# Squared-relu attention and an ELU feed-forward on one core: the lo*lo product of the scores is left out, and its neighbour runs as 64-row matmuls

## The chip, the cores and the metric

The kernel runs on one core of a Trainium2 chip. The metric is the device time of one execution in microseconds (us), lower is better. TensorE (PE) does the matrix products; each matmul instruction first loads its stationary operand, the weights (PEld). ScalarE (ACT) and VectorE (DVE) do the elementwise work, and SyncE's queue (SP) issues the DMA transfers. PSUM is the memory that TensorE writes: eight banks, each of 512 float32 values in each of 128 partitions.

## The reference

Four batches of 3008 tokens go through attention without softmax, and the 12032 tokens then through a feed-forward part with 2048 hidden units.

```python
scores = (1 / S) * z @ z.T            # z: 4 x 3008 x 64
attn = np.maximum(scores, 0.0) ** 2
x = u * (attn @ v)                    # u, v: 4 x 3008 x 256
h = x @ w_in                          # 256 x 2048, float64 weights
g = np.where(h > 0, h, np.exp(np.minimum(h, 0)) - 1)
out = g @ w_out                       # 2048 x 256
```

## The kernel before

Each float32 operand of a product is split into two float32r halves of 12 significant bits, hi + lo. A product of two operands is then hi\*hi + hi\*lo + lo\*hi, three matmuls that accumulate in PSUM.

The queries of a batch are cut into six blocks (four of 502, two of 500), 24 blocks in all; the keys into 12 pairs of 128-key chunks per block. A step is one pair of one block: 288 steps in attention. In a step, `a_front` makes the scores of the pair in one score tile `f` (two banks, one for each chunk), `a_mid` makes relu and square on ScalarE and splits the result into `hi` and `lo` on VectorE, and two steps later `a_back` multiplies them with the values `v` into an accumulator `acc` (two banks, d = 0 and 1), twelve matmuls. After a block's last pair (p = 11) VectorE multiplies the accumulator with `u`, and the result `x` goes to DRAM.

Scores have only 64 rows (z has 64 features), so hi and lo of a key chunk lie one under the other in `l`: rows 0 to 63 hold hi, rows 64 to 127 hold lo. The queries are held twice: `hh` has hi in both halves of the rows, `ll` has lo in both. One matmul of `l` with `hh` gives hi\*hi + lo\*hi, one with `ll` gives hi\*lo + lo\*lo.

The feed-forward part has 24 blocks of 8 steps: `m_front` (12 matmuls into a tile `h` of the same kind as `f`), `m_mid1` to `m_mid4` on ScalarE and VectorE, and three steps later `m_back` (12 matmuls into an accumulator `yacc`, copied out by ScalarE at the block's end).

The order of work is written out by hand: a loop over slots t issues, for each t, `a_front(t)`, `a_mid(t)`, background jobs of that slot, then `a_back(t - 2)`. Every engine's queue has its work in that order. The background jobs are the loads and splits of the next operands: `v_split` and `l_hi`, `l_lo` (in 12 slots around each batch's start), `r_split` (hh and ll of the next block), `w_split` (the weights' hi and lo, one VectorE operation per slot over 128 slots).

In PSUM, `f` and `acc` have two buffers each of two banks, which are all eight.

Of the kernel before, what the change touches and what calls it, by code (L numbers as in the profile page):

```python
# [7 lines left out]
F32 = mybir.dt.float32  # L8
# [2 lines left out]
AF = mybir.ActivationFunctionType  # L11
ALU = mybir.AluOpType

# Every float32 operand of a matrix product is split exactly into two float32r
# halves of 12 significant bits (hi + lo); a product is then hi*hi + hi*lo + lo*hi
# in three single-pass float32r matmuls that accumulate in float32.
BLOCKS = (502, 502, 502, 502, 500, 500)


# [1 line left out]
def relu2_attention_elu_mlp(  # L21
# [9 lines left out]
    nc = tc.nc  # L31
    B, D, S = uT.shape
    K = zz.shape[1] // 2
    DFF = w_in.shape[1]
    P = 128
    KD = D // P
    KF = DFF // P
# [9 lines left out]
    MS = KF // 2  # L47
# [7 lines left out]
    z1 = ctx.enter_context(tc.tile_pool(name="z1", bufs=1))  # L55
    p2 = ctx.enter_context(tc.tile_pool(name="p2", bufs=2))
    p3 = ctx.enter_context(tc.tile_pool(name="p3", bufs=3))
    ps = ctx.enter_context(tc.tile_pool(name="ps", bufs=2, space=bass.MemoryType.PSUM))
    dr = ctx.enter_context(tc.tile_pool(name="dr", bufs=1, space=bass.MemoryType.DRAM))

    wi_hi = res.tile([P, KD, DFF], F32R, name="wi_hi")
# [7 lines left out]
    def sub(lo, src, hi):  # L69
        nc.vector.tensor_tensor(out=lo, in0=src, in1=hi.bitcast(F32), op=ALU.subtract)  # L70

    def copy(out, in_):
        nc.scalar.activation(out=out, in_=in_, func=AF.Copy)  # L73
# [2 lines left out]
        copy(hi, src)  # L76
        sub(lo, src, hi)

# [1 line left out]
    v_raw, v_t = {}, {}  # L80

    def v_load(b, p):
# [13 lines left out]
        split(o[:, 0], o[:, 1], t)  # L96
        v_t[b, p] = o

# [1 line left out]
    l_raw, l_t = {}, {}  # L100

    def l_load(b, g, c0=0, c1=GW):
# [11 lines left out]
        copy(l_t[b, g][:, c0:c1], l_raw[b, g][:, c0:c1])  # L114

    def l_lo(b, g, c0=0, c1=GW):
        o = l_t[b, g][K:, c0:c1]
        sub(o, l_raw[b, g][K:, c0:c1], o)

# [1 line left out]
    r_raw, r_t = {}, {}  # L121

    def r_load(k):
# [18 lines left out]
        nc.sync.dma_start(out=t[:, :, :n], in_=uT[b, :, i0:i0 + n].rearrange("(c p) n -> p c n", p=P))  # L142
        u_t[k] = t

    # ---- float64 weights: hi = the sign, the exponent and 11 bits of the fraction,
    # lo = the next 24 bits of it, rounded to 12. The exponent is rebased by dropping
    # three of its bits, which a magnitude in float32's range determines; smaller
    # magnitudes become zero. ----
    UNIT = 512
    WARM = 7  # L150
    w_raw = {}
# [44 lines left out]
        yield  # L196
        stt(out=lo, in0=r, scalar=2.0 ** -35, in1=h.bitcast(F32), op0=ALU.mult, op1=ALU.mult)

# [1 line left out]
    def products(late):  # L200
        if late:
            return [(c, d, q) for c in range(2) for q in (0, 2, 1) for d in range(KD)]
        return [(c, d, q) for c in range(2) for d in range(KD) for q in range(3)]

# [1 line left out]
    x_d = {}  # L206
    f_t, e_t, acc_t = {}, {}, {}

    def a_front(s):
        k, p = divmod(s, NP)  # L210
        n, b = cols(k)[1:]
        t = ps.tile([P, 2, 512], F32, tag="f", name="f")
        hh, ll = r_t[k]
        for c in range(2):
            o = (p % 4) * 2 * P + c * P
            w = l_t[b, p // 4][:, o:o + P]
            nc.tensor.matmul(t[:, c, :n], w, hh[:, :n], start=True, stop=False)  # L217
            nc.tensor.matmul(t[:, c, :n], w, ll[:, :n], start=False, stop=True)  # L218
        f_t[s] = t

    def a_mid(s):
        k, p = divmod(s, NP)
# [13 lines left out]
    def a_back(s):  # L236
        k, p = divmod(s, NP)
        n, b = cols(k)[1:]
        hi, lo = e_t.pop(s)
        vt = v_t[b, p]  # L240
        if p == 0:
            acc_t[k] = ps.tile([P, KD, 512], F32, tag="acc", name="acc")
        acc = acc_t[k]
        for c, d, q in products(s < 2):
            end = p == NP - 1 and c == 1
            if end and q == 1:
                continue
            w = vt[:, q // 2, c, d * P:(d + 1) * P]
            g = (lo if q == 1 else hi)[:, c, :n]
            nc.tensor.matmul(acc[:, d, :n], w, g, start=(p == 0 and c == 0 and q == 0), stop=(end and q == 2))  # L250
        if p == NP - 1:
            u = u_t.pop(k)
            nc.vector.tensor_tensor(out=u[:, :, :n], in0=acc_t.pop(k)[:, :, :n], in1=u[:, :, :n], op=ALU.mult)
            x_d[k] = dr.tile([P, KD, n], F32, name=f"x{k}")
            nc.sync.dma_start(out=x_d[k], in_=u[:, :, :n])

# [1 line left out]
    xr_t, x_t, g_t, y_t = {}, {}, {}, {}  # L258

    def x_load(k):  # L260
# [13 lines left out]
    def m_front(s):  # L274
        k, m = divmod(s, MS)
        n = cols(k)[1]
        hi, lo = x_t[k]
        t = ps.tile([P, 2, 512], F32, tag="f", name="h")
        for c in range(2):
            f0 = (2 * m + c) * P  # L280
            for j in range(KD):
                wh, wl = wi_hi[:, j, f0:f0 + P], wi_lo[:, j, f0:f0 + P]
                o = t[:, c, :n]
                nc.tensor.matmul(o, wh, hi[:, j, :n], start=(j == 0), stop=False)  # L284
                nc.tensor.matmul(o, wh, lo[:, j, :n], start=False, stop=False)  # L285
                nc.tensor.matmul(o, wl, hi[:, j, :n], start=False, stop=(j == KD - 1))  # L286
        f_t[s] = t
# [10 lines left out]
        nc.scalar.activation(out=h[:, c0:c1, :n], in_=f[:, c0:c1, :n], func=AF.Copy)  # L298
        nc.vector.tensor_scalar(out=m[:, c0:c1, :n], in0=h[:, c0:c1, :n], scalar1=0.0, scalar2=None, op0=ALU.min)  # L299

    # exp(m) - 1 = (exp(m) + 1) * tanh(m / 2), which keeps its digits near zero
    def m_mid2(s, c0=0, c1=2):
        n = cols(s // MS)[1]
        _, m, t = g_t[s]
# [26 lines left out]
    def m_back(s):  # L331
        k, m = divmod(s, MS)
        i0, n, b = cols(k)
        hi, lo = e_t.pop(s)
        if m == 0:
            acc_t[k] = ps.tile([P, KD, 512], F32, tag="acc", name="yacc")
        acc = acc_t[k]
        late = s >= MSTEP - 2
        for c, d, q in products(late):
            f = 2 * m + c  # L340
            w = (wo_lo if q == 2 else wo_hi)[:, f, d * P:(d + 1) * P]
            g = (lo if q == 1 else hi)[:, c, :n]
            nc.tensor.matmul(  # L343
                acc[:, d, :n], w, g, start=(f == 0 and q == 0), stop=(f == KF - 1 and q == (1 if late else 2))
            )
        if m == MS - 1:
            del acc_t[k]
            y = vp.tile([P, KD, NB], F32, tag="v", name="y")
            t0 = b * S + i0
            if s < MSTEP - 1:  # L350
                copy(y[:, :, :n], acc[:, :, :n])
                nc.sync.dma_start(
                    out=outT[:, t0:t0 + n].rearrange("(c p) n -> p c n", p=P), in_=y[:, :, :n]
                )
            else:
                copy(y[:, 0, :n], acc[:, 0, :n])
                nc.vector.tensor_copy(out=y[:, 1, :n], in_=acc[:, 1, :n])
                nc.sync.dma_start(out=outT[:P, t0:t0 + n], in_=y[:, 0, :n])
                nc.scalar.dma_start(out=outT[P:, t0:t0 + n], in_=y[:, 1, :n])

# [1 line left out]
    jobs = {}  # L362

    def at(slot, fn, *a):
# [41 lines left out]
    with tc.manual_schedule():  # L406
        l_load(0, 0, 0, 2 * P)
        r_load(0)
        l_load(0, 0, 2 * P, GW)
        warm = p3.tile([P, 512], F32R, tag="hi", name="warm")  # L410
        nc.vector.memset(warm.bitcast(F32), 0.0)
        copy(p3.tile([P, 1], F32R, tag="lo", name="cwarm"), warm[:, :1].bitcast(F32))
        f = ps.tile([P, 2, 512], F32, tag="f", name="fwarm")
        for i in range(WARM):
            nc.tensor.matmul(f[:, i % 2], warm[:, :P], warm, start=True, stop=True)
        l_hi(0, 0, 0, 2 * P)
        l_lo(0, 0, 0, 2 * P)
        r_split(0)
        l_hi(0, 0, 2 * P, GW)
        l_lo(0, 0, 2 * P, GW)  # L420
        for t in range(-9, 0):
            background(t)
        for t in range(NSTEP + MSTEP + 3):
            s = t - NSTEP
            if s < 0:
                a_front(t)
                a_mid(t)
            elif s < MSTEP:
                m_front(s)
                m_mid1(s)  # L430
            if 2 <= s < MSTEP:
                m_mid4(s - 2)
            if 0 <= s < MSTEP:
                m_mid2(s)
            if 1 <= s < MSTEP - 1:
                m_mid3(s - 1)
            if s == MSTEP - 1:
                halves = (0, 1), (1, 2)
                for fn, k in (m_mid3, s - 1), (m_mid4, s - 1), (m_mid3, s), (m_mid4, s):
                    for c0, c1 in halves:  # L440
                        fn(k, c0, c1)
            background(t)
            if t >= 2 and s < 2:
                a_back(t - 2)
            if s >= 3:
                m_back(s - 3)
        assert not jobs, sorted(jobs)
# [32 lines left out]
```

## Time and profile before

| | us |
|---|---|
| three runs, median (lowest to highest) | 2108.54 (2108.49 to 2109.82) |
| the profiled execution's span, first to last instruction | 2107.8 |
| PE busy / PEld busy | 2097.8 / 1729.8 |
| DVE busy / ACT busy | 1533.2 / 1437.1 |
| granted TensorE clock, mean | 0.999 |

The span is that of the one execution that was profiled; it has no device time of its own beside it, and the median of the runs lies 0.7 us above the span. Busy time of PE counts each matmul to its modelled end, and these overlap, so the pace of the matmuls is read from their starts.

### The profile page before, as it was taken

What the parts mean: (1) busy time and instruction counts of PE and PEld (TensorE: products, weight loads), DVE (VectorE), ACT (ScalarE), POOL (GpSimd) and SP (SyncE); (2) the same over time, 40 slices, a digit from 0 to 9 for tenths busy, and PEclk for the clock granted to TensorE, in tenths of its full rate; (3) what the DMA queues carried; (4) which work ended last, traced back from release to release, by engine and by line L of the source; (5) the groups of instructions that cost most, each with busy time, mean ns of one, the idle gap of its engine ahead of it and who ended that gap; (6) DMA issues with size and microseconds to landing.
All of it is one profiled execution on the core that took longest, in us unless ns stands there. A gap on an engine that the chain in (4) does not pass through costs nothing.

```text
span 2107.8 us, 22966 instructions
## 1 busy us (share of the span) xinstructions
PE 2097.8 (100%) x9175; PEld 1729.8 (82%) x9175; DVE 1533.2 (73%) x1648; ACT 1437.1 (68%) x1481; POOL 0.2 (0%) x4
## 2 busy tenths in 40 slices
PE   9999999999999999999999999999999999999998
PEld 7888888888888888888888888888888888888887
DVE  6767777677765576555587877777777877778777
ACT  7555665556655576555577777777777777777776
POOL 0000000000000000000000000000000000000000
PEclk9999999999999999999999999999999999999999
DMA  4121321113110031000101000000000000010000
GB/s 129 41 63 45 95 65 62 45 43 102 58 49 25 25 103 55 31 25 25 40 22 38 20 20 20 28 32 20 20 20 32 28 20 20 20 37 23 20 10 20
DMA packets 44555, 84.18 MB, mean 40 GB/s; under 512 B 3872, under 2 KB 35744, under 8 KB 44448
## 3 DMA queue, kind: packets, MB, share of 16 engines
q1 hardware_dynamic: 44304, 82.46, 12.1%
q8 instruction: 71, 1.16, 0.2%
q14 instruction: 36, 0.29, 0.0%
q10 hardware_dynamic: 144, 0.26, 0.0%
HBM read 58.06 MB, written 24.64 MB: 39 GB/s over the span
## 4 chain that ended last, share of the span: by engine, by line
PE 98%; DVE 0%; ACT 0%; DMA 0%; issue 0%; SPq 0%; DVEq 0%; ACTq 0%
PE acc L250 37%; PE yacc L343 25%; PE h L286 8%; PE h L284 8%; PE h L285 8%; PE f L218 6%; PE f L217 6%; DMA lraw<-in_zz 0%; ACT ghi L326 0%; DVE glo L327 0%; DVE hc L314 0%; ACT hc L298 0%; ACT l L73 0%; DVE t L311 0%; ACT r L229 0%
## 5 line engine op out<-in xcount | busy, mean ns | idle before, releaser
L250 PE MATMUL acc<-hi,v 128*128 128x502 f32 (+1 forms) x2304 | 752.2, 391 | 1.8 <-DVE v L70 1.1
L228 ACT ACTIVATE r<-f 128x1004 f32<-128x1004 f32 (+1 forms) x288 | 290.6, 1009 | 382.2 <-PE f L218 381.5
L250 PEld LDWEIGHTS acc<-hi,v 128*128 128x128 f32 x2304 | 434.3, 189 | 94.0 <-DVE v L70 1.5
L230 DVE CAST hi<-r 128x1004 fp32r<-128x1004 f32 (+1 forms) x288 | 196.5, 682 | 329.6 <-ACT r L229 329.1
L250 PE MATMUL acc<-lo,v 128*128 128x502 f32 (+1 forms) x1104 | 429.6, 390 | 0.1
L298 ACT ACTIVATE hc<-h 128x1004 f32<-128x1004 f32 (+1 forms) x192 | 193.8, 1009 | 249.1 <-PE h L286 249.0
L70 DVE TENSOR_TENSOR lo<-r,hi 128x1004 fp32r<-128x1004 f32 (+1 forms) x288 | 346.6, 1204 | 10.1
L229 ACT ACTIVATE r<-r 128x1004 f32<-128x1004 f32 (+1 forms) x288 | 300.3, 1043 | 9.1
L343 PE MATMUL yacc<-ghi,wo_hi 128*128 128x502 f32 (+1 forms) x768 | 299.9, 391 | 0.8 <-ACT ghi L326 0.8
L343 PE MATMUL yacc<-ghi,wo_lo 128*128 128x502 f32 (+1 forms) x768 | 300.1, 392 | 0.0
L343 PE MATMUL yacc<-glo,wo_hi 128*128 128x502 f32 (+1 forms) x768 | 298.8, 390 | 0.6 <-DVE glo L327 0.6
L284 PE MATMUL h<-xhi,wi_hi 128*128 128x502 f32 (+1 forms) x768 | 299.2, 390 | 0.0
L285 PE MATMUL h<-xlo,wi_hi 128*128 128x502 f32 (+1 forms) x768 | 298.8, 389 | 0.0
L286 PE MATMUL h<-xhi,wi_lo 128*128 128x502 f32 (+1 forms) x768 | 298.7, 389 | 0.0
L327 DVE TENSOR_TENSOR glo<-hc,ghi 128x1004 fp32r<-128x1004 f32 (+2 forms) x194 | 231.4, 1193 | 46.7 <-ACT ghi L326 46.5
L299 DVE TENSOR_SCALAR m<-hc 128x1004 f32<-128x1004 f32 (+1 forms) x192 | 130.9, 682 | 169.5 <-ACT hc L298 169.5
L250 PEld LDWEIGHTS acc<-lo,v 128*128 128x128 f32 x1104 | 208.6, 189 | 44.7 <-DVE lo L70 0.5
L314 DVE SCALAR_TENSOR_TENSOR hc<-hc,t 128x1004 f32<-128x1004 f32 (+2 forms) x194 | 231.3, 1192 | 6.6
L311 DVE SCALAR_TENSOR_TENSOR t<-m,t 128x1004 f32<-128x1004 f32 (+2 forms) x194 | 229.9, 1185 | 0.0
L217 PE MATMUL f<-hh,l 128*128 128x502 f32 (+1 forms) x576 | 224.8, 390 | 1.0 <-DVE l L70 0.8
L218 PE MATMUL f<-ll,l 128*128 128x502 f32 (+1 forms) x576 | 224.9, 390 | 0.0
L306 ACT ACTIVATE m<-m 128x1004 f32<-128x1004 f32 (+1 forms) x192 | 200.6, 1045 | 6.1
(42 smaller groups left out, 1800.0 us busy)
## 6 DMA issues: line engine op xcount, KB each, us to landing
vraw<-in_v SPq DMA_DIRECT2D x44, 256.0 KB, 2.7
u<-in_uT SPq DMA_DIRECT2D x16, 502.0 KB, 4.7
x<-u SPq DMA_DIRECT2D x16, 502.0 KB, 3.5
xr<-x SPq DMA_DIRECT2D x16, 502.0 KB, 4.2
outT<-y SPq DMA_DIRECT2D x16, 502.0 KB, 3.5
wraw<-in_w_in SPq DMA_DIRECT2D x8, 512.0 KB, 4.3
wraw<-in_w_out SPq DMA_DIRECT2D x8, 512.0 KB, 3.4
rraw<-in_zz SPq DMA_DIRECT2D x16, 251.0 KB, 4.7
```

What stands on the lines that cost most here:

```text
L70: nc.vector.tensor_tensor(out=lo, in0=src, in1=hi.bitcast(F32), op=ALU.subtract)
L217: nc.tensor.matmul(t[:, c, :n], w, hh[:, :n], start=True, stop=False)
L218: nc.tensor.matmul(t[:, c, :n], w, ll[:, :n], start=False, stop=True)
L228: nc.scalar.activation(out=r[:, :, :n], in_=f[:, :, :n], func=AF.Relu, scale=1.0 / S)
L229: nc.scalar.activation(out=r[:, :, :n], in_=r[:, :, :n], func=AF.Square)
L250: nc.tensor.matmul(acc[:, d, :n], w, g, start=(p == 0 and c == 0 and q == 0), stop=(end and q == 2))
L284: nc.tensor.matmul(o, wh, hi[:, j, :n], start=(j == 0), stop=False)
L285: nc.tensor.matmul(o, wh, lo[:, j, :n], start=False, stop=False)
L286: nc.tensor.matmul(o, wl, hi[:, j, :n], start=False, stop=(j == KD - 1))
L314: nc.vector.scalar_tensor_tensor(out=h[:, c0:c1, :n], in0=h[:, c0:c1, :n], scalar=0.0, in1=t[:, c0:c1, :n], op0=ALU.max, op1=ALU.add)
L327: nc.vector.tensor_tensor(out=lo[:, c0:c1, :n], in0=g[:, c0:c1, :n], in1=hi[:, c0:c1, :n].bitcast(F32), op=ALU.subtract)
L343: nc.tensor.matmul(acc[:, d, :n], w, g, start=(f == 0 and q == 0), stop=(f == KF - 1 and q == (1 if late else 2)))
```

## The change

The lo\*lo part of the scores is left out. In `l` the odd chunks have their halves exchanged: lo in rows 0 to 63, hi in rows 64 to 127. The matmul with `hh` uses all 128 rows as before. The one with `ll` uses the 64 rows that hold hi: the upper half of the rows for an even chunk, the lower for an odd one, as two matmuls of 64 rows that stand next to each other and write different banks. The score matmuls of two pairs are issued together in every second slot, four with `hh`, then four with `ll`. Score tiles get three buffers (six banks). The accumulator is now one, as two tiles of one bank, `acc0` and `acc1`, for d = 0 and 1; in a block's first and last pair the products are ordered by d first. The multiplication with u and the copy of y are made for each d apart. Comments were removed.

```diff
-    ps = ctx.enter_context(tc.tile_pool(name="ps", bufs=2, space=bass.MemoryType.PSUM))
+    pf = ctx.enter_context(tc.tile_pool(name="pf", bufs=3, space=bass.MemoryType.PSUM))
+    pa = ctx.enter_context(tc.tile_pool(name="pa", bufs=1, space=bass.MemoryType.PSUM))
...
     def l_lo(b, g, c0=0, c1=GW):
-        o = l_t[b, g][K:, c0:c1]
-        sub(o, l_raw[b, g][K:, c0:c1], o)
+        for c in range(2):
+            rows = slice(K, P) if c == 0 else slice(0, K)
+            o = l_t[b, g][rows, c0:c1].rearrange("p (n two w) -> p n two w", two=2, w=P)[:, :, c]
+            x = l_raw[b, g][rows, c0:c1].rearrange("p (n two w) -> p n two w", two=2, w=P)[:, :, c]
+            sub(o, x, o)
...
-    def products(late):
+    def products(late, edge):
         if late:
             return [(c, d, q) for c in range(2) for q in (0, 2, 1) for d in range(KD)]
+        if edge:
+            return [(c, d, q) for d in range(KD) for c in range(2) for q in range(3)]
         return [(c, d, q) for c in range(2) for d in range(KD) for q in range(3)]
+    def acc_tiles(k):
+        acc_t[k] = [pa.tile([P, 512], F32, tag=f"acc{d}", name=f"acc{d}") for d in range(KD)]
...
     def a_front(s):
         k, p = divmod(s, NP)
         n, b = cols(k)[1:]
-        t = ps.tile([P, 2, 512], F32, tag="f", name="f")
         hh, ll = r_t[k]
-        for c in range(2):
-            o = (p % 4) * 2 * P + c * P
-            w = l_t[b, p // 4][:, o:o + P]
-            nc.tensor.matmul(t[:, c, :n], w, hh[:, :n], start=True, stop=False)
-            nc.tensor.matmul(t[:, c, :n], w, ll[:, :n], start=False, stop=True)
-        f_t[s] = t
+        work = []
+        for i in range(2):
+            f_t[s + i] = pf.tile([P, 2, 512], F32, tag="f", name="f")
+            for c in range(2):
+                o = ((p + i) % 4) * 2 * P + c * P
+                work.append((f_t[s + i][:, c, :n], l_t[b, (p + i) // 4][:, o:o + P], c))
+        for t, w, c in work:
+            nc.tensor.matmul(t, w, hh[:, :n], start=True, stop=False)
+        for t, w, c in work:
+            rows = slice(c * K, (c + 1) * K)
+            nc.tensor.matmul(t, w[rows], ll[rows, :n], start=False, stop=True)
...
         if p == NP - 1:
             u = u_t.pop(k)
-            nc.vector.tensor_tensor(out=u[:, :, :n], in0=acc_t.pop(k)[:, :, :n], in1=u[:, :, :n], op=ALU.mult)
+            del acc_t[k]
+            for d in range(KD):
+                nc.vector.tensor_tensor(out=u[:, d, :n], in0=acc[d][:, :n], in1=u[:, d, :n], op=ALU.mult)
...
-                copy(y[:, :, :n], acc[:, :, :n])
+                for d in range(KD):
+                    copy(y[:, d, :n], acc[d][:, :n])
...
             if s < 0:
-                a_front(t)
+                if t % 2 == 0:
+                    a_front(t)
                 a_mid(t)
```

On PE, two steps within the second block stood like this before (f, hh, ll, l: scores and their operands; hi, v: the products' operands; the number is the tile's):

```order
L250 MATMUL acc_179<-hi_357,v_363 128x502
L217 MATMUL f_438<-hh_107,l_238 128x502
L218 MATMUL f_438<-ll_108,l_238 128x502
L217 MATMUL f_438<-hh_107,l_238 128x502
L218 MATMUL f_438<-ll_108,l_238 128x502
L250 MATMUL acc_179<-hi_386,v_392 128x502
```

At each step, four score matmuls stand between twelve products and twelve products. On PE after the change, around the end of the second block (acc0_545 and acc1_546 are its accumulator, acc0_861 the next block's):

```order
L267 MATMUL acc1_546<-hi_771,v_461 128x502 x3
L233 MATMUL f_843<-hh_670,l_107 128x502 x2
L233 MATMUL f_844<-hh_670,l_107 128x502 x2
L236 MATMUL f_843<-ll_671,l_107 128x502 x2
L236 MATMUL f_844<-ll_671,l_107 128x502 x2
L267 MATMUL acc0_861<-hi_802,v_122 128x502
L267 MATMUL acc0_861<-lo_803,v_122 128x502
```

Eight score matmuls, the last four of 64 rows, now stand between the last product of one block and the first of the next, whose accumulator is the same memory. On DVE before, at the same block end (L230 and L70 split a pair's scores, L185 and L188 belong to the weights, L253 is the multiplication with u):

```order
L230 CAST hi_785<-r_784 128x1004
L70 TENSOR_TENSOR lo_786<-r_784,hi_785 128x1004
L185 TENSOR_SCALAR wtmp_739<-wraw_240 128x512
L230 CAST hi_810<-r_809 128x1004
L70 TENSOR_TENSOR lo_811<-r_809,hi_810 128x1004
L188 SCALAR_TENSOR_TENSOR wtmp_739<-wraw_240,wtmp_739 128x512
L253 TENSOR_TENSOR u_604<-acc_529,u_604 128x1004
```

On DVE after the change, at the same place (L272 is the multiplication):

```order
L247 CAST hi_802<-r_801 128x1004
L71 TENSOR_TENSOR lo_803<-r_801,hi_802 128x1004
L190 TENSOR_SCALAR wtmp_756<-wraw_253 128x512
L247 CAST hi_822<-r_821 128x1004
L71 TENSOR_TENSOR lo_823<-r_821,hi_822 128x1004
L193 SCALAR_TENSOR_TENSOR wtmp_756<-wraw_253,wtmp_756 128x512
L272 TENSOR_TENSOR u_616<-acc0_545,u_616 128x502
L272 TENSOR_TENSOR u_616<-acc1_546,u_616 128x502
```

The multiplication is two operations now, and both stand, as the one did, behind the splits of the next block's first two pairs (hi_802 and hi_822) and a weight operation after each. Of the 23 block ends that another attention block follows, eleven look like this; one, the first, has a v subtraction after the first split only; three, at the starts of batches, have it after both splits, and two l subtractions besides; eight have nothing.

## Rows read from the trace of the kernel before

**Rows 1.** The page, parts 1 and 4: span, busy time by engine, the last chain by line.
```profile
span 2107.8 us, 22966 instructions
...
PE 2097.8 (100%) x9175; PEld 1729.8 (82%) x9175; DVE 1533.2 (73%) x1648; ACT 1437.1 (68%) x1481; POOL 0.2 (0%) x4
...
PE acc L250 37%; PE yacc L343 25%; PE h L286 8%; PE h L284 8%; PE h L285 8%; PE f L218 6%; PE f L217 6%; DMA lraw<-in_zz 0%; ACT ghi L326 0%; DVE glo L327 0%; DVE hc L314 0%; ACT hc L298 0%; ACT l L73 0%; DVE t L311 0%; ACT r L229 0%
```

**Rows 2.** Windows of the two halves: window, length, busy us (records) by engine, PEclk, DMA share, GB/s.
```profile
20.48:1074.00 1053.52, 1053.22 (x4623) 870.29 (x4622) 707.09 (x853) 647.86 (x666) 0.00 (x0) 1.00 0.17 55
1074.00:2100.00 1026.00, 1025.41 (x4497) 846.76 (x4495) 812.31 (x778) 773.22 (x796) 0.00 (x0) 1.00 0.07 23
```

**Rows 3.** Timeline of one attention step, PE and ACT: start us, us, engine, line, operation.
```profile
129.31 0.39 PE L217 MATMUL f<-hh,l 128*128 128x502 f32 x1
...
129.99 0.40 PE L218 MATMUL f<-ll,l 128*128 128x502 f32 x1
...
130.23 0.39 PE L250 MATMUL acc<-hi,v 128*128 128x502 f32 x1
...
130.43 1.01 ACT L228 ACTIVATE r<-f 128x1004 f32<-128x1004 f32 x1 [1.57 <-PE f L218]
...
132.99 0.39 PE L217 MATMUL f<-hh,l 128*128 128x502 f32 x1
```

**Rows 4.** Groups of instructions, shapes apart: count, busy us, mean ns of one, idle before.
```profile
L218 PE MATMUL f<-ll,l 128*128 128x502 f32 x384 | 150.2, 391 | 0.0
...
L218 PE MATMUL f<-ll,l 128*128 128x500 f32 x192 | 74.6, 389 | 0.0
```

**Rows 5.** Timeline, two places where TensorE's weights were loaded after a wait.
```profile
10.97 0.30 PEld L250 LDWEIGHTS acc<-lo,v 128*128 128x128 f32 x2 [0.49 <-DVE lo L70]
10.97 0.72 PE L250 MATMUL acc<-lo,v 128*128 128x502 f32 x2
...
1062.13 0.50 PE L343 MATMUL yacc<-glo,wo_hi 128*128 128x502 f32 x1 [0.30 <-DVE glo L327]
...
1062.47 0.40 PE L343 MATMUL yacc<-ghi,wo_lo 128*128 128x502 f32 x1
```

**Rows 6.** Timeline, ScalarE and VectorE within the step of rows 3.
```profile
130.73 0.68 DVE L188 SCALAR_TENSOR_TENSOR wtmp<-wraw,wtmp 128x512 int32<-128x512 int32 x1
...
131.47 1.04 ACT L229 ACTIVATE r<-r 128x1004 f32<-128x1004 f32 x1
...
132.54 0.68 DVE L230 CAST hi<-r 128x1004 fp32r<-128x1004 f32 x1 [1.13 <-ACT r L229]
...
133.26 1.21 DVE L70 TENSOR_TENSOR lo<-r,hi 128x1004 fp32r<-128x1004 f32 x1
...
134.38 0.42 DVE L190 TENSOR_SCALAR wraw<-wraw 128x512 int32<-128x512 int32 x1
```

**Rows 7.** Timeline, ScalarE and VectorE at the start of the second batch.
```profile
269.43 0.62 ACT L73 ACTIVATE v<-vraw 128x512 fp32r<-128x512 f32 x1
...
269.95 1.05 ACT L73 ACTIVATE l<-lraw 128x1024 fp32r<-128x1024 f32 x1
...
271.08 1.01 ACT L228 ACTIVATE r<-f 128x1004 f32<-128x1004 f32 x1
...
275.75 0.69 DVE L70 TENSOR_TENSOR l<-lraw,l 64x512 fp32r<-64x512 f32 x1
...
276.47 1.20 DVE L253 TENSOR_TENSOR u<-acc,u 128x1000 f32<-128x1000 f32 x1
```

**Rows 8.** Groups of instructions, VectorE: a subtraction of half a pair's size.
```profile
L70 DVE TENSOR_TENSOR ll<-rraw,hh 128x502 fp32r<-128x502 f32 x16 | 10.8, 676 | 1.0 <-ACT hh L73 1.0
```

**Rows 9.** Timeline, ScalarE at the end of a feed-forward block.
```profile
1100.57 1.01 ACT L298 ACTIVATE hc<-h 128x1004 f32<-128x1004 f32 x1 [1.55 <-PE h L286]
...
1104.42 0.99 ACT L73 ACTIVATE y<-yacc 128x1004 f32<-128x1004 f32 x1
```

**Rows 10.** Timeline, ScalarE at the start of the program.
```profile
11.30 1.06 ACT L73 ACTIVATE l<-lraw 128x1024 fp32r<-128x1024 f32 x1 [2.35 <-DMA lraw<-in_zz]
```

More of the change, by code (lines that the diff above doesn't have):

```diff
@@ L241, in a_back @@
         if p == 0:
-            acc_t[k] = ps.tile([P, KD, 512], F32, tag="acc", name="acc")
+            acc_tiles(k)
         acc = acc_t[k]
-        for c, d, q in products(s < 2):
+        for c, d, q in products(s < 2, p in (0, NP - 1)):
             end = p == NP - 1 and c == 1
@@ L249, in a_back @@
             g = (lo if q == 1 else hi)[:, c, :n]
-            nc.tensor.matmul(acc[:, d, :n], w, g, start=(p == 0 and c == 0 and q == 0), stop=(end and q == 2))
+            nc.tensor.matmul(acc[d][:, :n], w, g, start=(p == 0 and c == 0 and q == 0), stop=(end and q == 2))
         if p == NP - 1:
             u = u_t.pop(k)
-            nc.vector.tensor_tensor(out=u[:, :, :n], in0=acc_t.pop(k)[:, :, :n], in1=u[:, :, :n], op=ALU.mult)
+            del acc_t[k]
+            for d in range(KD):
+                nc.vector.tensor_tensor(out=u[:, d, :n], in0=acc[d][:, :n], in1=u[:, d, :n], op=ALU.mult)
             x_d[k] = dr.tile([P, KD, n], F32, name=f"x{k}")
@@ L277, in m_front @@
         hi, lo = x_t[k]
-        t = ps.tile([P, 2, 512], F32, tag="f", name="h")
+        t = pf.tile([P, 2, 512], F32, tag="f", name="h")
         for c in range(2):
@@ L335, in m_back @@
         if m == 0:
-            acc_t[k] = ps.tile([P, KD, 512], F32, tag="acc", name="yacc")
+            acc_tiles(k)
         acc = acc_t[k]
         late = s >= MSTEP - 2
-        for c, d, q in products(late):
+        for c, d, q in products(late, m in (0, MS - 1)):
             f = 2 * m + c
@@ L343, in m_back @@
             nc.tensor.matmul(
-                acc[:, d, :n], w, g, start=(f == 0 and q == 0), stop=(f == KF - 1 and q == (1 if late else 2))
+                acc[d][:, :n], w, g, start=(f == 0 and q == 0), stop=(f == KF - 1 and q == (1 if late else 2))
             )
@@ L355, in m_back @@
             else:
-                copy(y[:, 0, :n], acc[:, 0, :n])
-                nc.vector.tensor_copy(out=y[:, 1, :n], in_=acc[:, 1, :n])
+                copy(y[:, 0, :n], acc[0][:, :n])
+                nc.vector.tensor_copy(out=y[:, 1, :n], in_=acc[1][:, :n])
                 nc.sync.dma_start(out=outT[:P, t0:t0 + n], in_=y[:, 0, :n])
@@ L412, in relu2_attention_elu_mlp @@
         copy(p3.tile([P, 1], F32R, tag="lo", name="cwarm"), warm[:, :1].bitcast(F32))
-        f = ps.tile([P, 2, 512], F32, tag="f", name="fwarm")
+        f = pf.tile([P, 2, 512], F32, tag="f", name="fwarm")
         for i in range(WARM):
```

## The prediction

> **What bounds the kernel now.** I read the page's first part, the span and the chain first: TensorE (PE) is busy 2097.8 of 2107.8 us, and the chain that ended last runs through its matmul lines [rows 1]. The windows by stage say the same of each half: attention has 1053.22 busy of 1053.52 us, feed-forward 1025.41 of 1026.00, at granted clock 1.00, the 2.4 GHz level [rows 2]. 1053.52 us over 4623 matmuls is 0.228 us from one start to the next; a record is longer (0.39) because it includes the way through the array. So the kernel is a stream of matmuls at 0.228 us, and a matmul that goes is worth that much, as long as nothing new makes PE wait. VectorE (DVE) is busy 707 us of the attention's 1053, ScalarE (ACT) 648 [rows 2]: room, but both follow PE in a chain, which matters below.
>
> The timeline of one step shows the part that changes: four score matmuls from 129.31 on, the twelve of an earlier pair from 130.23, the next step at 132.99; Relu starts 0.44 us after the last score matmul's start [rows 3].
>
> **What is removed.** L218's matmuls number 384 + 192 = 576 [rows 4]. Each becomes a 64-row matmul on half the array, and two of them (even and odd chunk, in different banks of one score tile) can stream together: 576 slots become 288, so 288 x 0.228 = **-65.7 us**. That is the ceiling.
>
> **What the half-array matmuls add.** Every second slot now holds four full matmuls, then four of 64 rows, then full ones again (the order listings): two changes of shape in each of 144 double fronts, 288 in all. The trace of before has no 64-row matmul, so I bound the price of a change. Below: nothing, if weights for the new shape are loaded ahead as they are now. Above: the array empties until the last record ends, 0.39 - 0.228 = 0.16 us, and the first weights are then loaded in the open. What a load in the open costs is visible where PE waited: the matmul at 1062.13 lasted 0.50 in place of 0.39, and its successor came 0.34 later in place of 0.228, so 0.11 us; two loads in a row take 0.30, so they follow each other at 0.11 [rows 5]. Together 0.27 us a change, 0.54 a double front.
>
> The Trainium skill, TensorEngine Tiling (Array Packing), Tiling Modes, Key Properties, says that changing the tiling mode drains TensorE. By that rule the sum would be that of the second rival below; no row here shows a drain.
>
> Four loads at 0.11 are 0.44 us, under the two slots (0.456) in which two pairs stream, so the loads alone need not stop the pairs. I take one load in the open for each change and no full emptying, 0.11, since that is a price that rows show, and it lies between the ends: 288 x 0.11 = **+31.7 us**. (Ends: 0 and 77.8.)
>
> **What one accumulator adds.** Before, two accumulators alternate, so the multiplication by u (L253) could come late. Now the next block's first product waits for it. I follow it, with t = 0 at the first product of the block's last pair but one (p = 10), whose double front, already the next block's first, has just ended. PE then needs 12 + 10 products (22 x 0.228 = 5.02), a change (0.11), six slots of scores (1.37) and a change (0.11): it wants the accumulator at **6.61**.
>
> DVE's way there, by the starts in [rows 3, 6]: the first tile's last score matmul starts two slots (0.46) and a change (0.11) before 0, its Relu 0.44 after that, at -0.13; Square at +0.91 (1.04 on); cast at 1.98 (1.07); subtraction at 2.70 (0.72); next DVE work at 3.82 (1.12). The second tile's Relu starts at 1.95, Square 2.99, cast at 4.06 at the earliest. Three cases, which the DVE order tells apart:
> - Eleven block ends have a weight-splitting operation after each subtraction (0.42 and 0.68 long). The first pushes the cast to 4.27; subtraction 4.99, second operation 6.11, multiplication 6.82 to 7.50 (a half with 502 columns, priced as the 0.68 us subtraction of that size [rows 8]). PE waits 0.89 and loads in the open, 0.11: 1.0 each, **11 us**.
> - Three block ends at a batch's start have ACT's v copy and l copy before the second Relu (0.52 + 1.13), and v and l subtractions on DVE [rows 7]: second Relu 3.60, cast 5.71, subtraction 6.43, v 7.55, l 8.26 (0.9 as two pieces), multiplication 9.16 to 9.84: 3.3 each, **10 us**. The very first block, with a v operation after the first subtraction, has about 0.6.
> - Eight have nothing else: cast 4.06, multiplication 5.90 to 6.58, just in time. Its cover is those 6.61 us of PE work; each 0.1 us that a change is cheaper uncovers about 0.1 here.
>
> The last block's second accumulator half is covered, since its first six products (1.37 us) lie ahead of it and a half takes 0.68. Sum **+21.5 us**. What is queued on DVE behind the multiplication is the next cast, with a pair of products (2.7 us) to spare. The store of x behind it on SP's queue is read only in the feed-forward half.
>
> **Edits at nothing.** The feed-forward also has one accumulator, emptied by two ACT copies. The one copy now starts 3.85 us after the Copy of h and takes 0.99 [rows 9]; PE needs the first half 5.3 us after that same start (its 12 products, begun 0.2 before it, and 12 more of the next front). Two halves, about 0.6 each by the v copy of 512 columns [rows 7], end at 4.5 and 5.1: covered by 0.8 us of PE's work. Without that cover a miss of 0.2 us at 23 block ends would cost 5 us. Three score buffers: the double front's tiles were read by Relu at least 4 us earlier. Lo subtractions of l in two halves: 24 more DVE operations, hidden in the 33% that DVE idles, except in the batch case above. At the start the first Relu comes some 2 us later, because four chunks' lo must be there; ACT waits 2.35 us for the l load soon after [rows 10], which absorbs it.
>
> **Sum.** -65.7 + 31.7 + 21.5 = -12.5 us on the span of 2107.8, so 2095.3; runs lie 0.7 above the span (median 2108.54), so **2096 us**.
>
> **Rivals.**
> - Cheap changes or early multiplications. If loads run ahead across a change (price 0), PE reaches the block end 0.22 sooner and DVE's chain starts 0.11 later: each of 15 waits grows by 0.33, the eight others by 0.3, 28.9 in all. -65.7 + 28.9 = -37: 2072. About the same comes if changes cost 0.11 and the block-end waits don't appear (-34: 2074.5). For it: today every load lies under the matmul before it [rows 3]. Against: loads under a matmul are shown only between equal shapes.
> - The emptied array, on the other side. At 0.54 a double front the changes cost 77.8, and a later PE leaves 14 of block-end waits: -65.7 + 77.8 + 14 = +26: 2135. It decides from about 0.32 a double front, where the sum is zero. For it: a record ends 0.16 after the next start, so something is in flight at each change. Against: a record's end is modelled, and nothing shows that a new shape must wait for it. The Trainium skill's rule on tiling modes, above, speaks for this one.
> - Not side by side. If the two halves stream one after the other, the saving is zero and the change doesn't do what it says: 31.7 + 14 or so on top, some 2150. For it: they share the way of weights and of scores out. Against: they use different rows and different banks.
>
> **How the numbers follow.** Forecast (2083 to 2104, a price of 0.12 to 0.29 a double front) 0.43; cheap or early 0.17; the emptied array, with its upper half from 2121 on, 0.18; a price in between, 2104 to 2121, 0.16; not side by side 0.06. The range goes from the one bound of the change's price to the other, 2070 to 2135; the likeliest case's own is 2083 to 2104. A change of 0.2% is 4.2 us, about what a measurement can tell: faster than 2104.3 holds the first two, less 0.02 at the border, 0.58; 2104.3 to 2112.7 has these 0.02 and 0.10 of the price in between, 0.12; slower has the rest, 0.30.
>
> **What would show it.** The start of the two halves of a pair: within 0.12 us of each other, and about 0.46 us for four; the two at 0.228 each would mean not side by side. The stretch from the last full score matmul to the first half one, and from the last half one to the first product: 0.34 each by my price, 0.23 if free, 0.5 if the array empties. First products of a block: released by L272 on DVE, about 1 us in the early blocks, 3 at batch starts, none in the last eight. The feed-forward half should stay at 1026 us. I am wrong if the changes cost more than 0.16 each, or if the waits at block ends are not there or spread to every block.

## The result and the profile after

The changed kernel takes 2119.62 us (median of 4 runs, 2117.71 to 2121.66) against 2108.61 for the kernel before: 1.0051 times as long, interval 1.0037 to 1.0065. It is slower by 11 us, where 12.5 us less were forecast. The span of the profiled execution grew by 9.8 us, from 2107.8 to 2117.6.

The page's first lines, and the chain by engine:

```profile
span 2117.6 us, 23041 instructions
...
PE 2094.3 (99%) x9175; PEld 1655.8 (78%) x9175; DVE 1532.4 (72%) x1696; ACT 1424.1 (67%) x1504; POOL 0.2 (0%) x4
...
PE 93%; DVE 3%; ACT 2%; issue 1%; DMA 0%; SPq 0%; ACTq 0%; DVEq 0%
```

Against [rows 1], where PE's lines add up to 98% of the chain, PE has 93% now: some 6% belong to DVE, ACT and issue (issue is time in which an engine waited for nothing that the profile shows). The windows by half (columns as in [rows 2]) show where:

```profile
20.00:1085.00 1065.00, 1050.82 (x4626) 797.90 (x4625) 707.57 (x900) 634.90 (x668) 0.00 (x0) 1.00 0.17 54
1085.00:2110.00 1025.00, 1024.30 (x4492) 846.01 (x4490) 811.66 (x778) 774.09 (x818) 0.00 (x0) 1.00 0.07 23
```

The feed-forward half still has no idle time on PE (1024.30 of 1025.00 us). In the attention half PE is idle for 14 us, and the first feed-forward matmul starts at 1055.5 us, before at 1045.5: all of the loss lies in attention. A double front in the timeline, the counterpart of [rows 3]:

```profile
113.70 1.07 PE L233 MATMUL f<-hh,l 128*128 128x502 f32 x4
...
114.70 0.30 PEld L236 LDWEIGHTS f<-ll,l 64*128 64x128 f32 x4 [0.36 <-issue]
114.70 0.73 PE L236 MATMUL f<-ll,l 64*128 64x502 f32 x4
...
115.36 0.19 PEld L267 LDWEIGHTS acc<-hi,v 128*128 128x128 f32 x1 [0.36 <-issue]
115.36 0.50 PE L267 MATMUL acc<-hi,v 128*128 128x502 f32 x1
...
115.71 0.39 PE L267 MATMUL acc<-lo,v 128*128 128x502 f32 x1
```

Four full score matmuls start at 113.70, four of 64 rows at 114.70, the first product at 115.36 and the second at 115.71. A narrow window of the same timeline, before the second two halves have started:

```profile
114.70 0.19 PEld L236 LDWEIGHTS f<-ll,l 64*128 64x128 f32 x2 [0.36 <-issue]
114.70 0.50 PE L236 MATMUL f<-ll,l 64*128 64x502 f32 x2
```

Two half matmuls, and the loads of their weights, start at the same instant; the whole four last 0.73 us, as two full ones in a row do ([rows 5], 0.72). So the pairs do stream side by side. But from 113.70 to 115.71 seven slots of work (four full ones, two pairs, one product) take 2.01 us, where 7 x 0.228 = 1.60 was due: the two changes cost 0.41 us here. The fourth full matmul starts at 113.70 + 3 x 0.228 = 114.38, the first half weights are loaded 0.32 after it and not under it, and the matmul's record is 0.50 in place of 0.39. So each change has about 0.09 us in which nothing new starts (0.32 - 0.228) and then 0.11 of a load in the open. The way back shows the same: the last two halves start at 115.43 - 0.39 = 115.04, the first product 0.32 later, again with a record of 0.50, and the second product 0.35 after that. Over the starts of all 144 double fronts the medians are 0.32 for the stretch before each change's first matmul and 0.33 for the one behind it, which makes 0.195 a change and 0.39 a double front. I read the 0.09 as the array emptying; the trace shows the delay, not its reason.

The chain of waits, with the time in total, the number of waits and the longest, names two things on PE's side, the changes and the accumulator:

```profile
PEld f L236 <- issue: 50.6, 144, 0.4
...
PEld acc L267 <- issue: 40.9, 114, 0.4
PEld acc L267 <- DVE u L272: 23.1, 23, 3.3
PE acc L267 <- DVE u L272: 13.8, 14, 2.9
```

Each change has its idle time before a weight load, put down to issue (0.36 us a time, where 0.04 lies between two hidden loads). The last two rows are the accumulator. The one for weight loads counts all 23 block ends, also nine whose first product comes at the usual 0.32 us behind the last half; the one for matmuls has the 14 that made PE wait. Its 13.8 us count idle time beyond the modelled ends of the records; by the starts the waits are 14.8 us. The timeline at a block end in the weight-splitting part:

```profile
186.72 0.72 PE L236 MATMUL f<-ll,l 64*128 64x500 f32 x4
187.21 1.26 DVE L272 TENSOR_TENSOR u<-acc,u 128x502 f32<-128x502 f32 x2
...
187.95 0.50 PE L267 MATMUL acc<-hi,v 128*128 128x500 f32 x1 [0.50 <-DVE u L272]
...
188.28 0.39 PE L267 MATMUL acc<-lo,v 128*128 128x500 f32 x1
```

The last half matmuls stand at 186.72, the first product of the next block at 187.95, which is 1.23 after them in place of the 0.66 of 114.70 to 115.36: a wait of 0.57 us, ended by the first half of L272. Eleven block ends look like this. At the start of the second batch, one of three such places:

```profile
273.49 0.73 PE L236 MATMUL f<-ll,l 64*128 64x502 f32 x4
...
275.56 0.34 SPq L89 DMA_DIRECT2D vraw<-in_v  x1
275.56 0.85 DVE L71 TENSOR_TENSOR l<-lraw,l 64x256 fp32r<-64x256 f32 x2
...
276.34 1.25 DVE L272 TENSOR_TENSOR u<-acc,u 128x500 f32<-128x500 f32 x2
...
277.06 0.79 PE L267 MATMUL acc<-hi,v 128*128 128x502 f32 x1 [2.84 <-DVE u L272]
...
277.64 0.62 PE L267 MATMUL acc<-lo,v 128*128 128x502 f32 x1
277.64 0.75 PEld L267 LDWEIGHTS acc<-hi,v 128*128 128x128 f32 x2
278.06 1.04 PE L267 MATMUL acc<-hi,v 128*128 128x502 f32 x2
...
280.48 0.62 PE L267 MATMUL acc<-hi,v 128*128 128x502 f32 x2
```

Here the wait for L272 is 2.84 us by its row (277.06), and the products after it follow each other at 0.42 us (277.64, 278.06) until some 280 us, where 0.228 returns. Windows of that stretch, of the two other batch starts, and of the 250 us before the first of them; PEclk is the third number from the right:

```profile
273.00:280.00 7.00, 4.16 (x14) 2.85 (x13) 6.88 (x10) 5.63 (x7) 0.00 (x0) 0.78 0.43 134
...
541.00:547.00 6.00, 5.35 (x17) 4.35 (x18) 5.51 (x10) 2.98 (x4) 0.00 (x0) 0.72 0.73 224
803.00:810.00 7.00, 5.16 (x16) 4.15 (x17) 6.18 (x11) 3.97 (x5) 0.00 (x0) 0.76 0.60 177
20.00:270.00 250.00, 247.96 (x1098) 187.41 (x1096) 179.91 (x242) 153.78 (x166) 0.00 (x0) 1.00 0.23 73
```

The granted clock is 0.78, 0.72 and 0.76 in the three stretches and 1.00 before them, with four of the 0.57 us waits in that time: around each long wait part of the time is spent at the lower of the two levels (1.2 GHz), at which a product takes 0.42 us. In all 22 matmuls start at about that distance, which costs 4.3 us.

### The profile page after: what moved, and what is told of

Its sections match the earlier page's. It is cut to its first block, busy times and chain, and to the rows that moved or that the text cites. A ratio compares the mean times of both kernels' runs of the same rounds, so it can differ in the third digit from the quotient of the medians.

```text
span 2117.6 us, 23041 instructions
## 1 busy us (share of the span) xinstructions
PE 2094.3 (99%) x9175; PEld 1655.8 (78%) x9175; DVE 1532.4 (72%) x1696; ACT 1424.1 (67%) x1504; POOL 0.2 (0%) x4
## 4 chain that ended last, share of the span: by engine, by line
PE 93%; DVE 3%; ACT 2%; issue 1%; DMA 0%; SPq 0%; ACTq 0%; DVEq 0%
PE acc L267 35%; PE acc L362 25%; PE h L303 8%; PE h L305 8%; PE h L304 8%; PE f L233 5%; PE f L236 4%; ACT r L246 1%; ACT r L245 1%; DVE hi L247 1%; DVE u L272 0%; DMA lraw<-in_zz 0%; DVE lo L71 0%; ACT ghi L345 0%; DVE l L71 0%
## 5 line engine op out<-in xcount | busy, mean ns | idle before, releaser
L267 PE MATMUL acc<-hi,v 128*128 128x502 f32 (+1 forms) x2304 | 746.2, 399 | 15.3 <-DVE u L272 13.8
L362 PE MATMUL acc<-ghi,wo_hi 128*128 128x502 f32 (+1 forms) x768 | 299.8, 391 | 0.5 <-ACT ghi L345 0.5
L362 PE MATMUL acc<-ghi,wo_lo 128*128 128x502 f32 (+1 forms) x768 | 300.0, 391 | 0.0
L362 PE MATMUL acc<-glo,wo_hi 128*128 128x502 f32 (+1 forms) x768 | 299.0, 390 | 0.6 <-DVE glo L346 0.6
L345 ACT ACTIVATE ghi<-hc 128x1004 fp32r<-128x1004 f32 (+2 forms) x194 | 199.1, 1026 | 5.1 <-DVE hc L333 5.1
L324 ACT ACTIVATE t<-m 128x1004 f32<-128x1004 f32 (+1 forms) x192 | 198.2, 1032 | 1.9 <-DVE m L318 1.9
```

The lines of the kernel that those rows point to most:

```text
L267: nc.tensor.matmul(acc[d][:, :n], w, g, start=(p == 0 and c == 0 and q == 0), stop=(end and q == 2))
L362: nc.tensor.matmul(acc[d][:, :n], w, g, start=(f == 0 and q == 0), stop=(f == KF - 1 and q == (1 if late else 2)))
```

## The experiments

The theory after the result: the saving of 65.7 us is there; 288 changes of shape cost about 0.2 us each; the one accumulator costs some 15 us of waits at block ends. Rival A: the halves don't run side by side, and the changes cost nothing. Rival B: the changes cost nothing, and the accumulator eats all.

| kernel | us | kernel before, same chip | ratio, 95% interval |
|---|---|---|---|
| e1, full rows again | 2123.88 | 2109.32 | 1.0069 (1.0055 to 1.0082) |
| e2, multiplication first | 2099.69 | 2109.32 | 0.9954 (0.9941 to 0.9968) |
| e3, four changes a double front | 2160.2 | 2109.32 | 1.0242 (1.0223 to 1.026) |
| e4, all halves on the same rows | 2172.28 | 2109.32 | 1.0299 (1.028 to 1.0318) |
| e5, e2 and three pairs at a time | 2086.84 | 2108.86 | 0.9895 (0.9878 to 0.9911) |
| e6, halves alone, one pair at a time | 2153.88 | 2108.86 | 1.0213 (1.0193 to 1.0234) |
| e7, e5 with two pairs in the first block | 2082.25 | 2108.41 | 0.9872 (0.9856 to 0.9889) |

**e1: the second score matmul with all rows again.**

```diff
-            rows = slice(c * K, (c + 1) * K)
-            nc.tensor.matmul(t, w[rows], ll[rows, :n], start=False, stop=True)
+            nc.tensor.matmul(t, w, ll[:, :n], start=False, stop=True)
```

> The changed kernel with one thing undone: the second score matmul takes all 128 rows again (lo*lo comes back), so no change of shape and no saving; two pairs at a time, three score buffers and the one accumulator stay. Theory (the saving of 65.7 us is there, the 288 changes of shape cost about 0.21 us each, and the one accumulator costs 15 us of waits at 14 block ends): PE again has eight slots of scores between two blocks (6.84 us, as now with the changes), so the waits stay at 15 us: 2108.6 + 15, 2123 us, no idle time before half-row loads. Rival A (half matmuls do not run side by side and changes are free): also about 2123, but with the same pace per step as the changed kernel in the trace. Rival B (changes are free, the accumulator eats the whole 65 us): 2170 or more.

Measured 14.6 us above the kernel before, 2123.9, as the theory had it. The chain of waits has no row of issue ahead of a score load any more, and this one:

```profile
PE acc L266 <- DVE u L271: 10.3, 14, 2.6
```

That idle time, the weight loads in the open behind it, and the lower clock after the three longest waits are the price of the one accumulator by itself: without any saving it makes the kernel 0.7% slower. Rival B, which wanted 65 us, falls. The order of the score matmuls is the same as in the changed kernel, so the 0.195 us belong to the change of shape and not to the order.

**e2: the multiplication first.** At the 23 block ends the last pair's products and the multiplication are issued ahead of the next pair's relu, square and splits.

```diff
                 if t % 2 == 0:
                     a_front(t)
+                if t > NP and t % NP == 1:
+                    a_back(t - 2)
                 a_mid(t)
...
-            if t >= 2 and s < 2:
+            if t >= 2 and s < 2 and not (s < 0 and t > NP and t % NP == 1):
                 a_back(t - 2)
```

> The changed kernel, with the last pair's products and the multiplication with u issued ahead of the next pair's relu, square and splits in the slots in which a block ends (23 of them); PE's own order is the same. VectorE then multiplies as soon as the products are there, at about 4.1 us after the double front, and PE wants the accumulator at 6.8. Theory: the 15 us of waits at block ends go, 2119.6 - 15 = 2105 us, between 2102 and 2107, some 0.2% under the kernel before. Rival B (the accumulator's waits eat nearly all of the saving, the changes cost nothing): 2050 or less. A further rival: the late cast moves the wait to the block's second pair, no gain: 2118.

Measured 2099.7: 20 us under the changed kernel, 5 more than expected and 2 below the expected range, and 0.46% under the kernel before. The timeline at a block end:

```profile
140.52 0.42 DVE L200 TENSOR_SCALAR wtmp<-wi_hi 128x512 int32<-128x512 int32 x1
...
140.86 0.68 DVE L272 TENSOR_TENSOR u<-acc,u 128x502 f32<-128x502 f32 x1
...
141.99 0.68 DVE L272 TENSOR_TENSOR u<-acc,u 128x502 f32<-128x502 f32 x1 [0.45 <-PE acc L267]
142.59 0.67 DVE L247 CAST hi<-r 128x1004 fp32r<-128x1004 f32 x1
...
142.79 0.73 PE L236 MATMUL f<-ll,l 64*128 64x502 f32 x4
...
143.46 0.50 PE L267 MATMUL acc<-hi,v 128*128 128x502 f32 x1
...
143.79 0.39 PE L267 MATMUL acc<-lo,v 128*128 128x502 f32 x1
```

L272 now starts at 140.86 and 141.99, before the second cast, and the first product (143.46) follows the half matmuls (142.79) after 0.67 us: no wait. Of the 5 us that the theory lacked, 4.3 are the lower clock after the three long waits, which goes with them: this trace has no such matmul at the batch starts. What is left is the price of the changes alone: 2099.7 - 2109.3 + 65.7 = 56 us, 0.195 each, as the starts gave it.

**e3: four changes in a double front.** Two full, two half, two full, two half.

```diff
-        for t, w, c in work:
-            nc.tensor.matmul(t, w, hh[:, :n], start=True, stop=False)
-        for t, w, c in work:
-            rows = slice(c * K, (c + 1) * K)
-            nc.tensor.matmul(t, w[rows], ll[rows, :n], start=False, stop=True)
+        for pair in (work[:2], work[2:]):
+            for t, w, c in pair:
+                nc.tensor.matmul(t, w, hh[:, :n], start=True, stop=False)
+            for t, w, c in pair:
+                rows = slice(c * K, (c + 1) * K)
+                nc.tensor.matmul(t, w[rows], ll[rows, :n], start=False, stop=True)
```

> The changed kernel with the eight score matmuls of a double front in another order: two full, two half, two full, two half. The same work, four changes of shape in place of two, 288 more in all. Theory: 288 x 0.21 = 60 us more, less about 6 of waits at block ends that the longer front covers: 2170 to 2176 us. Rival A or B (changes are free): 2118 to 2121 us.

Measured 2160.2, 41 us more than the changed kernel and 10 under the expected range. Free changes are out. The miss has two parts: 0.195 a change gives 56, not 60; and the longer front covers more of the block-end waits, which keep 4.6 of 13.8 us on PE by the chain of waits, and no product at the lower clock there. 56 - 9 - 4 = 43.

**e4: all halves on rows 0 to 63.** An odd chunk then has lo\*lo in place of hi\*lo.

```diff
-            rows = slice(c * K, (c + 1) * K)
+            rows = slice(0, K)
```

> The changed kernel with all four half matmuls of a double front on rows 0 to 63, so that no two can run side by side; an odd chunk then has lo*lo in place of hi*lo. The number of matmuls and of changes is the same. Theory (pairs stream together now): the four take four slots, two more, 144 x 0.456 = 66 us, less 6 to 7 us of waits at block ends: 2177 to 2186 us. Rival A (they stream one after the other now): 2119 us, no change.

Measured 2172.3, 53 us more than the changed kernel, 5 below the expected range. Two slots more are 64 us by the starts (0.44 a front); the longer front covers the eleven short waits and part of the three long ones (the multiplication holds PE up three times, 6.2 us by the chain of waits, not 13.8), and the lower clock follows two of the three. 64 - 8 - 1.4 = 55. The timeline of a double front:

```profile
120.09 1.07 PE L233 MATMUL f<-hh,l 128*128 128x502 f32 x4
...
121.10 1.19 PE L236 MATMUL f<-ll,l 64*128 64x502 f32 x4
```

The four halves last 1.19 us (0.73 on both halves of the array), as four slots with a load in the open would: 0.11 + 3 x 0.228 + 0.39. Side by side is real, and rival A falls.

**e5: three pairs at a time**, with e2's order.

```diff
-        for i in range(2):
+        for i in range(3):
             f_t[s + i] = pf.tile([P, 2, 512], F32, tag="f", name="f")
...
-                if t % 2 == 0:
+                if t % 3 == 0:
                     a_front(t)
```

> The changed kernel with the multiplication with u issued first at block ends, and with three pairs at a time in place of two: six full score matmuls, six half ones, every third slot, in the same three score buffers. 96 fronts in place of 144, so 192 changes of shape. Theory (0.21 us a change): 96 x 0.21 x 2 = 40 in place of 60.5 us, 20 less than the same kernel with two pairs, if that lands at 2105: 2085 us, 2080 to 2092. No front stands between a block's last pair and the next block's first one, so the accumulator is wanted after 1.14 us; a wait of up to 0.5 us at 23 ends would add 11. Rival (the cost is not in the changes): no gain over two pairs.

Measured 2086.8, 1.1% under the kernel before and as expected: 96 fewer changes are worth 96 x 0.195 = 19 us over e2, and 13 of them arrived. Most of the rest is lost at the start, in the timeline of PE:

```profile
27.80 1.07 PE L233 MATMUL f<-hh,l 128*128 128x502 f32 x4
31.97 0.85 PE L233 MATMUL f<-hh,l 128*128 128x502 f32 x2 [3.10 <-DVE l L71]
```

The third triple front has its first four matmuls at 27.80 and the fifth at 31.97, after 3.10 us of waiting for the lo of the next l group, which a front of two needs two slots later. The granted clock is 0.66 from 32 to 37 us. The waits at block ends that were feared for this version are not there: the chain of waits has no row for the multiplication.

**e6: the half matmuls alone**, one pair at a time on the kernel before, with its two score buffers and two accumulators (`l_lo` as in the change).

```diff
+        w = [l_t[b, p // 4][:, (p % 4) * 2 * P + c * P:][:, :P] for c in range(2)]
         for c in range(2):
-            o = (p % 4) * 2 * P + c * P
-            w = l_t[b, p // 4][:, o:o + P]
-            nc.tensor.matmul(t[:, c, :n], w, hh[:, :n], start=True, stop=False)
-            nc.tensor.matmul(t[:, c, :n], w, ll[:, :n], start=False, stop=True)
+            nc.tensor.matmul(t[:, c, :n], w[c], hh[:, :n], start=True, stop=False)
+        for c in range(2):
+            rows = slice(c * K, (c + 1) * K)
+            nc.tensor.matmul(t[:, c, :n], w[c][rows], ll[rows, :n], start=False, stop=True)
```

> The kernel before with the half-row matmuls alone: one pair at a time, two score buffers, two accumulators, as before. 288 fronts, 576 changes. Theory (0.21 us a change, no wait at block ends): -65.7 + 576 x 0.21 = +55 us: 2160 to 2168 us. Rival A (no side by side, free changes): 2108 us. Rival B (free changes, all is lost at the one accumulator): 2043 us.

Measured 45 us above the kernel before, 6 below the expected range: (45 + 65.7) / 576 = 0.192 a change, the second measurement of the same price as in e2. Both rivals, at 2108 and 2043 us, fall. The timeline of a front:

```profile
118.01 0.62 PE L220 MATMUL f<-hh,l 128*128 128x502 f32 x2
...
118.56 0.49 PE L223 MATMUL f<-ll,l 64*128 64x502 f32 x2
...
118.98 0.49 PE L255 MATMUL acc<-hi,v 128*128 128x502 f32 x1
...
119.31 0.39 PE L255 MATMUL acc<-lo,v 128*128 128x502 f32 x1
```

From 118.01 to 119.31, 1.30 us for four slots (0.91): 0.39 for two changes, the same as in a double front. The price goes by the change, not by how much work stands between.

**e7: three pairs at a time after the first block**, with e2's order.

```diff
-    def a_front(s):
+    def a_front(s, pairs):
...
-        for i in range(2):
+        for i in range(pairs):
...
-                if t % 2 == 0:
-                    a_front(t)
+                pairs = 2 if t < NP else 3
+                if t % pairs == 0:
+                    a_front(t, pairs)
```

> The kernel with three pairs at a time and the multiplication first, but with two pairs at a time in the first block, where the triple front waited 3.1 us for the lo of l at 32 us and about 2 us more before it. Theory (0.195 us a change of shape, from the runs with one, two and four changes a front; no wait at block ends): 6 double and 92 triple fronts, 196 changes, 38.2 us; -65.7 + 38.2 = -27.5 us on the kernel before, 2081 us, 2079 to 2084. Rival (the 6 us that the triple kernel is above its sum are spread over all fronts, not in the first block): 2086 to 2088 us, no gain.

Measured 2082.25, 1.28% under the kernel before and 1 us from the sum. A triple front in the timeline:

```profile
206.96 1.52 PE L233 MATMUL f<-hh,l 128*128 128x500 f32 x6
208.41 0.94 PE L236 MATMUL f<-ll,l 64*128 64x500 f32 x6
```

Six halves follow six full matmuls after 1.45 us: five slots (1.14) and then 0.31 in place of 0.228 up to the first half. The rival, a loss spread over all fronts, falls. This is the fastest version tried.

## Why the prediction was wrong

- **What bounds the kernel: right.** PE's stream sets the time; feed-forward didn't move.
- **The saving of 65.7 us: right.** The trace shows the pairs start together, and e4 what they cost when they can't.
- **The price of a change: the step that failed.** I wrote "I take one load in the open for each change and no full emptying, 0.11". The load in the open is there, at 0.11; but before it there is a delay of about 0.09 more, which I had put at nothing, and the sum is 0.195 (e2) or 0.192 (e6). The term was 56 us, not 31.7, and that turned the sign. It lies between the bounds (0 and 0.27), nearer to the upper one, and over the 0.16 that I had named as the sign of being wrong. The delay is less than the whole end of a record (0.09, not 0.16). The Trainium skill, TensorEngine Tiling (Array Packing), Tiling Modes, Key Properties, says that changing the tiling mode drains TensorE. The trace agrees in that a delay stands at each change: 0.32 us from the last full matmul's start to the first half load, and as much on the way back where nothing else is waited for. I gave the two cases above my price 0.34, and the time fell into the lower of them, "a price in between".
- **The sign that I gave for the price: misread.** I had expected 0.34 us from the last full score matmul to the first half one by my price, and 0.32 came, as if I had been right. But a record whose load is in the open begins with that load ([rows 5]: 0.50 long, its successor 0.34 later). A load alone would have left that stretch at 0.228 and made only the start behind it late, 0.33. Both are late, so both have to be read.
- **The waits at block ends: right in place and cause, too large.** Eleven of 0.57 (forecast 1.0), three of 2.7 to 2.9 (forecast 3.3), the first block's of none (forecast 0.6), eight of none (forecast none), 14.8 us against 21.5. Part of it is the dearer change, which gives DVE more time. What I lacked is the lower clock after the three long ones, 4.3 us. That the two misses nearly cancel (19.1 against 21.5) is luck. -65.7 + 56 + 14.8 + 4.3 = +9.4, and the span grew by 9.8.
- **Edits at nothing: right.** The feed-forward's one accumulator has no wait in the trace, and the start costs nothing that shows.
- **The rival on the other side** (it decides from 0.32 a double front) named what I had left out, a wait at each change besides the load, with too high a price: 0.39, not 0.54.

## What to carry to other kernels

Half-array matmuls that stream side by side pay only by the group: here a group's two changes of shape cost 0.39 us, as much as 1.7 slots, so one pair at a time loses 0.7 slot a pair, two win 0.15 and three win 0.43. Whoever pays for a larger group with a buffer has to move the work that the buffer had covered: e2's reordering of one multiplication was worth more than the whole forecast gain. Where a price is bounded from both sides and the sign of the sum changes between the bounds, the sum has no sign yet: 0.11 gave -12.5 us, the middle of the bounds, 0.135, would still have given about -5, and 0.195 was measured. The part of a price that a row happens to show is not the whole price; here e6, the half matmuls without the other edits, measures it by itself.

## What the runs showed of the hardware

- A change between 128-row and 64-row matmuls costs 0.195 us (e2; 0.192 in e6): about 0.09 in which nothing new starts, and a weight load of 0.11 that is no longer hidden.
- Two 64-row matmuls on different halves of the rows run at the same time: four last 0.73 us, and 1.19 when all are on the same half (e4). The Trainium skill, TensorEngine Tiling (Array Packing), Tiling Modes, Key Properties, says that different tiles can load weights and multiply in parallel. The trace agrees: two 64-row loads, at different halves, take 0.19 us together (114.70), as one full load alone does (115.36).
- Each wait of 2.7 to 2.9 us on PE in the changed kernel was followed by seven or eight matmuls at 0.42 us in place of 0.228, at a lower granted clock: about 1.4 us, half as much again as the wait itself. The waits of 0.57 us left the clock at 1.00. In e4, with three waits of 2.0 to 2.4 us by the starts, the five microseconds behind the first two have a granted clock of 0.66 and 0.67, those behind the third 1.00.
